# Softmax denominators handled four units at a time, with DMA gathering and spreading them

## The chip, the cores and the metric

The kernel runs on one core of a Trainium2 chip. The metric is device time in microseconds (us). Three runs of the kernel before took 253.03, 253.61 and 254.1 us; the median is 253.61. Engines are named as the profile names them: PE (matrix), DVE (vector), ACT (scalar), POOL (GpSimd), SP (the engine that issues the DMAs). PSUM is the memory that PE writes, SBUF the working memory.

## What is computed

An adaLN block on 2048 tokens of width 512. A sliding-window attention with 32 heads of 16 dimensions comes first, then a token-mixing MLP of width 1792:

```python
mod = (silu(c) @ w_mod).reshape(1, 6, 1, 512)        # sa, ca, ga, sb, cb, gb
h = layernorm(x) * (1 + ca) + sa
q, k, v = split(h @ wqkv)                            # 32 heads of 16
p = softmax(mask(q @ k.T / 4))                       # a token sees itself and the 255 before it
x = x + ga * ((p @ v) @ wo)
h = layernorm(x) * (1 + cb) + sb
u = gelu(einsum('bsd,sf->bdf', layernorm(h), w1) + b1)
x = x + gb * (einsum('bdf,fs->bds', u, w2) + b2).T
```

## The kernel before, in words

**Tiling.** Tokens go in four groups G of 512, each of two halves H of 256 tokens (so H runs from 0 to 7). The 32 heads go in four sets g8 of eight. A *unit* is one half with one head set; there are 32 units. The scores of the units are cut into 75 *chunks*; units share chunks, five chunks for a pair of units (L438). The names below are the operation names in the code, and they are used in the prediction.

**One chunk** (L1161). `S`: PE writes scores for four heads into three PSUM banks (`pss`, one buffer) and a fourth (`psb`, two buffers). `EA`, `EB`: ACT takes the exponential of `pss` (1536 columns) and of `psb` (512) into the SBUF tile `et` (`E_BUFS` = 7 buffers). `M`: DVE multiplies parts of `et` by a mask.

**One unit** (L1229, L1265). When its last chunk is masked, `AV`: PE makes the weighted values and, with a block of constants (`ones_bd`, L303), the denominators. Both go into one PSUM bank `po`: columns 0 to 255 the values, columns 256 to 511 the denominators, each repeated over the 16 partitions of its head. Then `ln` and `rz` on ACT give 1/denominator as exp(-ln z) in the SBUF tile `lz` (128x256 each), and `OT` on DVE multiplies the values in PSUM by it. `OT` frees the bank. There are three such banks (`od`), shared with every projection and with the MLP.

**Around it.** `proj(G)` (L866): the layernorm of x (`l1st` statistics on DVE, `l1ag` eight small steps on POOL, `xn` the normalization), a transposing DMA `xt`, scale and shift `h1T`, then matmuls k, q, v. Each result is copied out of PSUM (`ke`, `qe`, `ve`) and laid out by `kk` (K), `vo` and `vp` (V; `vp` after a DMA `vx`). `post(G)` (L1023): the output projection `wo` on PE, `x2` adds x, `l2st`, `l2ag`, `n2` (normalize), `m2` (two tensor operations: times cb, plus sb), `l3st`, `l3ag`, `hb` (normalize again, into the tiles `hb` that the MLP reads). `partials()` (L1090): the pieces `p` of the first MLP matmul that need only the tokens of groups 0 and 1: `p0` to `p19` need the `hb` tiles of group 0, `p20` to `p55` also those of group 1. `pe` and `pd` take them out of PSUM. `tail()` (L1328): the rest of the first matmul (`u`), the activation, and the second matmul (`py`), whose weights are loaded behind everything else.

**What sets the order.** All operations are created first and numbered in the order of creation. The list `ORDER` (L62) is a permutation of these numbers, and every engine executes its own operations in that order, SP's DMA issues too. Operations that may go on more than one engine take the engine under which `CHOSEN` (L118) lists their number. Both lists are constants. The costs in the code (the numbers in `op(...)`) choose PSUM banks and cost nothing at run time.

**Broadcast vectors** (L541). `bc`: for each of four vectors, four matmuls with a stationary tile in which silu(c) is repeated over 128 columns, into a bank of its own. `bce`: one DVE instruction each into `bc_ga`, `bc_cb1`, `bc_sb`, `bc_gb`.

Of the kernel before, what the change touches and what calls it, by code (L numbers as in the profile page):

```python
# [22 lines left out]
NG = 4  # L23
# [36 lines left out]
E_BUFS = 7  # L60
LOG = None
ORDER = [  # L62
# [54 lines left out]
]  # L117
CHOSEN = {  # L118
    "ACT": [
        47, 48, 50, 51, 74, 82, 1062,  # L120
    ],
    "DVE": [
# [5 lines left out]
    ],  # L128
    "POOL": [
# [86 lines left out]
def kernel(  # L216
# [324 lines left out]
    for n, (v, dst) in enumerate(((2, bc_ga), (4, bc_cb1), (3, bc_sb), (5, bc_gb))):  # L541
        def e_bc(n, v=v):
            if n == 0:
                box["bc", v] = bank([P, D], F32, "ps_b")
# [890 lines left out]
```

## Time and profile before

| | us |
|---|---|
| median of three runs | 253.61 |
| span of the profiled execution, first to last instruction | 252.3 |
| PE busy | 235.3 |
| DVE busy | 205.4 |
| ACT busy | 179.5 |
| POOL busy | 126.3 |

The run list gives no time of its own for the profiled execution. Its span lies 1.3 us under the median of the runs, and a run's time also holds what lies around the span. Nearly all instructions go through one helper line (L256), so groups in the profile are told apart by their tiles: `et<-pss` is `EA`, `et<-psb` is `EB`, `et<-et,maskt` is `M`, `lz<-po` is `ln`, `lz<-lz` is `rz`, `OT<-po,lz` is `OT`, `KT<-kb,mask_par` is `kk`, `VT<-vb` and `VT<-vs` are `vo` and `vp`. A view of windows gives the busy time of each engine in stretches of the span. The granted PE clock is 1.00 in all of them.

### The profile page before, as it was taken

To read this page: it belongs to the slowest core of one execution; us is meant where nothing else is said; L and a number is where in the kernel's file an instruction comes from. 1 tells how busy PE (TensorE), PEld (TensorE's weight loads), DVE (VectorE), ACT (ScalarE), POOL (GpSimd) and SP (SyncE) were. 2 spreads that over 40 slices of the span, in tenths; PEclk is the share of its full clock that TensorE was granted. 3 is DMA by queue.
4 is the path that set the end of the run, shared out by engine and by line. 5 is a ranking of instruction groups with operands and counts; after the bars stand their busy time and mean duration, and the time that the engine had idled before them with its cause. 6 is when DMAs were issued, how large, how long until landed. Compare 5 with 4: busy or idle time off the path is not lost.

```text
span 252.3 us, 9189 instructions
## 1 busy us (share of the span) xinstructions
PE 235.3 (93%) x3949; PEld 126.0 (50%) x3949; DVE 205.4 (81%) x408; ACT 179.5 (71%) x254; POOL 126.3 (50%) x228
## 2 busy tenths in 40 slices
PE   7988888899987889999999999999999999999995
PEld 2656644445554544555546454556444444444443
DVE  5499998989989998999897999999978764444443
ACT  4699998999999999999999999997147510000000
POOL 8268968795899989845886348173000000000000
PEclk9999999999999999999999999999999999999999
DMA  6999364356055200003401536314999201111111
GB/s 200 323 351 294 48 47 86 44 70 187 3 74 112 53 23 3 4 3 104 131 3 45 155 82 189 105 44 113 343 388 386 108 22 43 44 52 52 42 44 42
DMA packets 42625, 28.13 MB, mean 111 GB/s; under 512 B 12376, under 2 KB 38488, under 8 KB 42584
## 3 DMA queue, kind: packets, MB, share of 16 engines
q1 hardware_dynamic: 42576, 27.54, 39.4%
q8 instruction: 31, 0.51, 0.9%
q14 instruction: 10, 0.08, 0.1%
q10 hardware_dynamic: 8, 0.00, 0.0%
HBM read 22.03 MB, written 2.10 MB: 96 GB/s over the span
## 4 chain that ended last, share of the span: by engine, by line
PE 52%; ACT 24%; DVE 7%; DMA 5%; issue 5%; POOL 4%; SPq 1%; POOLq 0%; DVEq 0%
ACT et L256 20%; PE py L256 19%; PE pu L256 16%; PE po L256 5%; PE pss L256 5%; ACT lz L256 3%; PE pa L256 3%; DMA x<-in_A_x_dram 2%; DVE et L256 2%; DMA h1T<-xn 2%; DMA wmod<-in_w_mod_dram 1%; POOL h1T L256 1%; PE pq L256 1%; DVE st L256 1%; PE pk L256 1%
## 5 line engine op out<-in xcount | busy, mean ns | idle before, releaser
L256 ACT ACTIVATE et<-pss 128x1536 bf16<-128x1536 f32 x75 | 110.7, 1476 | 2.8 <-PE psb L256 2.3
L256 PE MATMUL py<-guT,w2r 128*128 128x512 bf16 (+2 forms) x238 | 48.7, 366 | 0.0
L256 ACT ACTIVATE et<-psb 128x512 bf16<-128x512 f32 x75 | 46.9, 626 | 0.0
L256 DVE TENSOR_TENSOR et<-et,maskt 128x1024 bf16<-128x1024 bf16 (+2 forms) x79 | 46.4, 603 | 0.1
L256 PE MATMUL pu<-hb,w1s 128*32 128x512 bf16 (+1 forms) x302 | 39.0, 380 | 0.2 <-DVE QT L256 0.2
L256 PEld LDWEIGHTS <-w2r 128*128 128x128 bf16 x238 | 22.8, 98 | 26.1 <-issue 0.3
L256 PE MATMUL pss<-QT,KT 32*128 32x64 bf16 (+3 forms) x720 | 29.9, 230 | 6.2 <-ACT et L256 3.5
L256 PE MATMUL po<-et,VT 128*32 128x64 bf16 (+3 forms) x960 | 32.2, 234 | 1.3 <-DVE kb L256 0.6
L256 PE MATMUL po<-et,ones_bd 128*32 128x256 bf16 (+3 forms) x624 | 31.7, 268 | 0.0
L256 PEld LDWEIGHTS <-KT 32*128 32x128 bf16 x960 | 17.1, 92 | 28.5 <-issue 24.6
L256 DVE TENSOR_TENSOR otile<-py,xr 128x512 bf16<-128x512 f32 (+2 forms) x17 | 11.2, 660 | 24.4 <-PE py L256 24.2
L256 POOL TENSOR_SCALAR KT<-kb,mask_par 128x512 bf16<-128x512 bf16 (+1 forms) x36 | 25.0, 707 | 11.4 <-DVE kb L256 11.1
L256 PE MATMUL psb<-QT,KT 32*128 32x64 bf16 (+3 forms) x240 | 29.3, 231 | 0.0
L256 PEld LDWEIGHTS <-VT 128*32 128x32 bf16 x960 | 20.8, 96 | 13.2 <-issue 4.7
L256 PE MATMUL pk<-h1T,wqkv 128*32 128x512 bf16 (+4 forms) x228 | 21.1, 340 | 2.4 <-DVE OT L256 1.0
L256 DVE BATCH_NORM_STATS2 st<-x 128x6 f32<-128x512 bf16 x32 | 21.5, 680 | 2.1 <-DMA x<-in_A_x_dram 2.1
L256 PEld LDWEIGHTS <-wqkv 128*32 128x32 bf16 (+1 forms) x350 | 15.3, 96 | 12.7 <-issue 4.7
L256 PEld LDWEIGHTS <-w1s 128*32 128x32 bf16 (+1 forms) x302 | 14.1, 97 | 15.0 <-issue 1.5
L256 PE MATMUL pv<-wqkv,h1T 128*32 128x512 bf16 (+2 forms) x202 | 17.1, 348 | 1.3 <-DVE OT L256 0.7
L256 PE MATMUL pu<-hb,w1r 128*128 128x512 bf16 (+1 forms) x96 | 17.9, 380 | 0.0
L256 PE MATMUL pa<-wod,OT 128*32 128x512 bf16 (+1 forms) x136 | 17.2, 381 | 0.0
L256 PEld LDWEIGHTS <-ones_bd 128*32 128x32 bf16 x624 | 15.8, 97 | 0.1
(109 smaller groups left out, 350.1 us busy)
## 6 DMA issues: line engine op xcount, KB each, us to landing
w2r<-in_B_w_dram SPq DMA_DIRECT2D x14, 512.0 KB, 10.2
w1s<-in_B_w_dram SPq DMA_DIRECT2D x19, 256.0 KB, 4.0
w1r<-in_B_w_dram SPq DMA_DIRECT2D x9, 256.0 KB, 4.3
x<-in_A_x_dram SPq DMA_DIRECT2D x16, 128.0 KB, 5.2
wmod<-in_w_mod_dram SPq DMA_DIRECT2D x4, 512.0 KB, 7.8
out_dram<-otile SPq DMA_DIRECT2D x15, 128.0 KB, 1.7
wmod<-in_w_mod_dram SPq DMA_DIRECT2D x4, 256.0 KB, 3.9
wqkv<-in_A_wqkv_dram SPq DMA_DIRECT2D x4, 256.0 KB, 5.7
```

Of the source, the lines that this page charges most:

```text
L256: ins = call(*args, **kwargs)
```

## The change

Units are finished in batches. All but the last two units go through it: seven batches of four units and one of two.

- `ev` (DVE or ACT) copies the whole bank, values and denominators, to the SBUF tile `ev` (128x512 float32, six buffers) and frees the bank.
- `zg` (a DMA) gathers the eight distinct rows of denominators of the unit into eight rows of the tile `zc`.
- After the fourth `zg` of a batch, one `ln` and one `rz` on ACT work on the 32 rows of `zc`.
- `zb` (a DMA for each unit) spreads each of the eight rows over 16 partitions, back into `ev`.
- `OT` (DVE or POOL) multiplies the two halves of `ev`, both in SBUF.

The last two units keep `ln`, `rz` and the multiply from PSUM. The four broadcast vectors are made by sixteen matmuls of 32 columns, four side by side, into one bank; one `bce` scales them, and four DMAs `bb` spread them over the partitions. To make room in SBUF, `et` has six buffers in place of seven, some tiles move to pools that are released earlier, and the last four `hb` tiles are made only when the weights of the projections are released.

`ORDER` and `CHOSEN` are new throughout. Counted by name, these operations change their number or their engine:

| operation | before | after |
|---|---|---|
| `OT` | DVE 32 | DVE 10, POOL 22 |
| `ev` | none | DVE 28, ACT 2 |
| `ln` and `rz` | ACT 64 | ACT 20 |
| `zg`, `zb`, `bb` | none | SP 64 |
| `bce` | DVE 4 | DVE 1 |
| `xn` | DVE 7, POOL 9 | DVE 4, POOL 12 |
| `n2` | DVE 8, POOL 8 | DVE 6, POOL 10 |
| `m2` | DVE 12, POOL 4 | DVE 11, POOL 5 |
| `vo` | DVE 2, POOL 10 | POOL 12 |
| `vp` | POOL 16 | DVE 1, POOL 15 |
| `kk` | DVE 1, POOL 18 | DVE 2, POOL 17 |
| `pe` | DVE 13, ACT 1 | DVE 11, ACT 3 |
| `ve` | DVE 16 | DVE 15, ACT 1 |

```diff
-E_BUFS = 7
+E_BUFS = 6
+EV_BUFS = 6
...
+    zc = const.tile([P, HQ], F32, name="zc")
...
+    def e_bc(n):
+        if n == 0:
+            box["bc"] = bank([P, D], F32, "ps_b")
+        for k in (2 * n, 2 * n + 1):
+            for i, (v, _) in enumerate(vectors):
                 te.matmul(
-                    box["bc", v][:], lhsT=sT_rep[:, k, :], rhs=wmod[:, k, v * D : (v + 1) * D],
-                    start=(k == 0), stop=(k == ND - 1),
+                    box["bc"][32 * i : 32 * i + 32, :], lhsT=sT_rep[:, k, :], rhs=wmod[:, k, v * D : (v + 1) * D],
+                    start=(k == 0), stop=(k == ND - 1), tile_position=(0, 32 * i), skip_group_check=True,
                 )
...
+        def e_bb(e, n=n, dst=dst):
+            dma.dma_start(out=dst[:], in_=bcs[32 * n : 32 * n + 32, :].unsqueeze(1).to_broadcast([32, ND, D]))
...
     def finish(unit, i):
...
+        def e_o(e):
+            ENGINE[e].tensor_tensor(
+                out=OT[G % 2][g8][:, (Hh % 2) * HQ : (Hh % 2 + 1) * HQ],
+                in0=(unit["ps"] if direct else unit["ev"])[:, 0, :], in1=unit["ev"][:, 1, :], op=ALU.mult,
+            )
...
+        def e_ev(e):
+            e_new()
+            copy(e, unit["ev"][:], unit["ps"][:])
+
+        def e_zg(e):
+            dma.dma_start(out=zc[rows, :], in_=unit["ev"][0 : P : DH, 1, :])
+
+        def e_zb(e):
+            dma.dma_start(out=unit["ev"][:, 1, :], in_=zc[rows, :].unsqueeze(1).to_broadcast([8, DH, HQ]))
+
+        a = op("ev", {"DVE": 0.6, "ACT": 0.5}, 0.6, e_ev, deps=[av], pos=i + LZ_POS)
+        unit["avs"][0].frees = [a]
+        g = op("zg", "SP", 0.5, e_zg, deps=[a], pos=i + LZ_POS, extra=0.2)
...
+        def e_bln(e):
+            ac.activation(out=zc[own, :], in_=zc[own, :], func=ACT.Ln)
+
+        def e_brz(e):
+            ac.activation(out=zc[own, :], in_=zc[own, :], func=ACT.Exp, scale=-1.0)
...
+            z = op("zb", "SP", 0.5, e_spread, deps=[b], pos=at + LZ_POS, extra=1.2)
+            spread.append(z)
+            d = mult_ops[u["H"], u["g8"]] = op("OT", {"DVE": 0.34, "POOL": 0.8}, 0.34, e_mult, deps=[z], pos=at + OT_POS)
```

From the new `ORDER`, the parts that the prediction uses. POOL, from the `l3ag` of group 0 to that of group 1: `l3ag0 hb1 hb2 OT10 kk15 OT15 vp12 vp13 OT12 vo8 kk14 vo9 l2ag1 n26 n24 n25 m26 kk16 m24 vo11 OT16 vp15 kk18 vo10 kk17 vp14 l3ag1 hb5 hb4`. The same stretch before: `l3ag0 kk13 kk12 hb3 vp10 hb0 kk14 vo6 hb2 vp11 l2ag1 n24 n27 m26 m27 l3ag1 vo8 kk15 hb5 vp13 hb7`. PE after: `... S41 AV48 AV49 p6 S42 p7 p0 p1 S43 ...` and `... S60 p20 AV70 p21 p44 S61 ...`; before: `... S42 AV45 AV46 p0 p1 S43 ...` and `... S55 ... S56 p20 p21 ...`. Numbers behind a name count its operations from 0 in the order of creation (so `S42` is the 43rd chunk).

More of the change, by code (lines that the diff above doesn't have):

```diff
@@ L274 @@
     xres = [xpool.tile([P, D], BF, name=f"x{t}") for t in range(NT)]
-    hb = [xpool.tile([P, D], BF, name=f"hb{t}") for t in range(NT)]
+    hb = [xpool.tile([P, D], BF, name=f"hb{t}") for t in range(NT - ND)]
     identity = const.tile([P, P], BF, name="identity")
@@ L306 @@
     nc.gpsimd.memset(ones_bd[KB:P, DH : 2 * DH], ZSCALE)
-    nothing = const.tile([P, D], BF, name="nothing")
-    nc.vector.memset(nothing[:], 0.0)
     late = ctx.enter_context(tc.tile_pool(name="late", bufs=2))
@@ L318 @@
     VT = [kvpool.tile([P, 8, DH, 2 * DH], BF, name=f"VT{r}") for r in range(3)]
-    work = att.enter_context(tc.tile_pool(name="work", bufs=2))
     epool = att.enter_context(tc.tile_pool(name="epool", bufs=E_BUFS))
@@ L335 @@
     modw = tc.alloc_tile_pool(name="modw", bufs=1, side="right")
-    warm = nothing
+    warm = nothing = modw.tile([P, D], BF, name="nothing")
+    nc.vector.memset(nothing[:], 0.0)
     wmod = modw.tile([P, ND, 6 * D], BF, name="wmod")
@@ L473 @@
     sT = modw.tile([P, ND], BF, name="sT")
-    sT_rep = modw.tile([P, ND, P], BF, name="sT_rep")
+    sT_rep = modw.tile([P, ND, 32], BF, name="sT_rep")
+    bcs = modw.tile([P, D], BF, name="bcs")
+    bc_fix = modw.tile([P, 2], F32, name="bc_fix")
+    nc.gpsimd.memset(bc_fix[:, 0:1], 1.0)
+    nc.gpsimd.memset(bc_fix[0:32, 0:1], ZSCALE)
+    nc.gpsimd.memset(bc_fix[:, 1:2], 0.0)
+    nc.gpsimd.memset(bc_fix[32:64, 1:2], 1.0)
     box = {}
@@ L504 @@
     o5.frees = [o6]
-    o_rep = op("sTrep", "DVE", 0.35, lambda e: ve.tensor_copy(
-        out=sT_rep[:], in_=sT[:].unsqueeze(2).to_broadcast([P, ND, P])), deps=[o6], pos=-6, ready=15.0)
+    o_rep = op("sTrep", "DVE", 0.15, lambda e: ve.tensor_copy(
+        out=sT_rep[:], in_=sT[:].unsqueeze(2).to_broadcast([P, ND, 32])), deps=[o6], pos=-6, ready=15.0)
     def e_fm(k):
@@ L652 @@
     transposed = {}
+    placed = []
     def proj0():
@@ L781, in e_kb @@
             def e_kb(e):
-                box["kb", g8] = work.tile([P, D], BF, name="kb", tag=kb_tag, bufs=1)
+                box["kb", g8] = wpool.tile([P, D], BF, name="kb", tag=kb_tag, bufs=1)
                 copy(e, box["kb", g8][:, 0 : 2 * P], box["kq", g8][:, 0, :])
@@ L823, in e_ve @@
             def e_ve(e):
-                box["vb", tb] = work.tile([P, 2, 256], BF, name="vb", tag=vb_tag, bufs=1)
+                box["vb", tb] = wpool.tile([P, 2, 256], BF, name="vb", tag=vb_tag, bufs=1)
                 copy(e, box["vb", tb][:], box["v", tb][:])
@@ L953, in e_ke @@
                 else:
-                    box["kb", g8] = work.tile([P, D], BF, name="kb", tag=kb_tag, bufs=1)
+                    box["kb", g8] = wpool.tile([P, D], BF, name="kb", tag=kb_tag, bufs=1)
                     copy(e, box["kb", g8][:], box["k", g8][:])
@@ L982, in e_ve @@
             def e_ve(e):
-                vb = box["vb", tb] = work.tile([P, 2, 256], BF, name="vb", tag=vb_tag, bufs=1)
+                vb = box["vb", tb] = wpool.tile([P, 2, 256], BF, name="vb", tag=vb_tag, bufs=1)
                 copy(
@@ L989, in e_vx @@
             def e_vx(e):
-                vs = box["vs", tb] = work.tile([P, 256], BF, name="vs", tag=vs_tag, bufs=1)
+                vs = box["vs", tb] = wpool.tile([P, 256], BF, name="vs", tag=vs_tag, bufs=1)
                 dma.dma_start(out=vs[0:KB, :], in_=box["vb", tb][KB:P, 0, :])
@@ L1011, in v @@
             b = op("vp", {"POOL": 0.78, "DVE": 0.45}, 0.78, lambda e: e_vp(e, False), deps=[vx] + war + zeros[r3], pos=pos)
+            placed.extend([own, b])
             slot(vb_tag, ve_op, own, vx)
@@ L1102, in e_rel @@
             box["B"] = ctx.enter_context(tc.tile_pool(name="partB", bufs=1, side="right"))
+            hb.extend(box["B"].tile([P, D], BF, name=f"hb{t}") for t in range(NT - ND, NT))
         for n in range(NF // 2):
@@ L1267, in finish @@
         av = av_ops[G, g8] = unit["avs"][-1]
-        lz_tag = turn("lz")
-        def e_ln(e):
-            unit["lz"] = late.tile([P, HQ], F32, name="lz", tag=lz_tag, bufs=1)
-            ac.activation(out=unit["lz"][:], in_=unit["ps"][:, 1, :], func=ACT.Ln)
-        def e_rz(e):
-            ac.activation(out=unit["lz"][:], in_=unit["lz"][:], func=ACT.Exp, scale=-1.0)
+        tag = turn("ev", EV_BUFS)
+        direct = Hh == 2 * NG - 1 and g8 >= 2
+        members = box.setdefault("batch", [])
@@ L1277, in e_o, with e_new @@
+        def e_new():
+            unit["ev"] = kvpool.tile([P, 2, HQ], F32, name="ev", tag=tag, bufs=1)
         def e_o(e):
-            ve.tensor_tensor(
+            ENGINE[e].tensor_tensor(
                 out=OT[G % 2][g8][:, (Hh % 2) * HQ : (Hh % 2 + 1) * HQ],
-                in0=unit["ps"][:, 0, :], in1=unit["lz"][:], op=ALU.mult,
+                in0=(unit["ps"] if direct else unit["ev"])[:, 0, :], in1=unit["ev"][:, 1, :], op=ALU.mult,
             )
-        a = op("ln", "ACT", 0.26, e_ln, deps=[av], pos=i + LZ_POS)
@@ L1284, in finish, with e_ln, e_rz @@
-        b = op("rz", "ACT", 0.31, e_rz, deps=[a], pos=i + LZ_POS)
-        d = mult_ops[Hh, g8] = op("OT", "DVE", 0.34, e_o, deps=[b], pos=i + OT_POS)
-        unit["avs"][0].frees = [d]
-        slot(lz_tag, a, d)
+        if direct:
+            def e_ln(e):
+                e_new()
+                ac.activation(out=unit["ev"][:, 1, :], in_=unit["ps"][:, 1, :], func=ACT.Ln)
+            def e_rz(e):
+                ac.activation(out=unit["ev"][:, 1, :], in_=unit["ev"][:, 1, :], func=ACT.Exp, scale=-1.0)
+            a = op("ln", "ACT", 0.26, e_ln, deps=[av], pos=i + LZ_POS)
+            b = op("rz", "ACT", 0.31, e_rz, deps=[a], pos=i + LZ_POS)
+            d = mult_ops[Hh, g8] = op("OT", "DVE", 0.34, e_o, deps=[b], pos=i + OT_POS)
+            unit["avs"][0].frees = [d]
+            slot(tag, a, d)
+            return
@@ new lines, in finish @@
+        unit["avs"][0].frees = [a]
+        g = op("zg", "SP", 0.5, e_zg, deps=[a], pos=i + LZ_POS, extra=0.2)
+        members.append((unit, i, tag, a, g, e_o, e_zb))
+        if len(members) < (2 if Hh == 2 * NG - 1 else 4):
+            return
+        own = slice(32 * (box["batches"] % 4), 32 * (box["batches"] % 4) + 8 * len(members))
+        def e_bln(e):
+            ac.activation(out=zc[own, :], in_=zc[own, :], func=ACT.Ln)
+        def e_brz(e):
+            ac.activation(out=zc[own, :], in_=zc[own, :], func=ACT.Exp, scale=-1.0)
@@ new lines, in finish @@
+        n = box["batches"]
+        a = op("ln", "ACT", 0.26, e_bln, deps=[m[4] for m in members], pos=i + LZ_POS)
+        slot(f"zc{n % 4}", members[0][4])
+        b = op("rz", "ACT", 0.31, e_brz, deps=[a], pos=i + LZ_POS)
+        spread = []
+        for u, at, tag, first, g, e_mult, e_spread in members:
+            z = op("zb", "SP", 0.5, e_spread, deps=[b], pos=at + LZ_POS, extra=1.2)
+            spread.append(z)
+            d = mult_ops[u["H"], u["g8"]] = op("OT", {"DVE": 0.34, "POOL": 0.8}, 0.34, e_mult, deps=[z], pos=at + OT_POS)
+            slot(tag, first, d)
@@ L1289 @@
+        tenants[f"zc{n % 4}"] = spread
+        box["batches"] += 1
+        box["batch"] = []
     for G in range(NG):
```

38 lines of the change are left out of this document (17 added, 21 removed), and 128 rows, old and new, of tables (CHOSEN, ORDER).

## The prediction

> **What bounds the kernel now.** I read the share of busy time first, then three stretches, then the chain that ended last to see which engine carries each.
>
> ```profile
> span 252.3 us, 9189 instructions
> PE 235.3 (93%) x3949; PEld 126.0 (50%) x3949; DVE 205.4 (81%) x408; ACT 179.5 (71%) x254; POOL 126.3 (50%) x228
> ```
>
> ```profile
> core 0: us, PE busy (x) PEld busy (x) DVE busy (x) ACT busy (x) POOL busy (x), PEclk, DMA share, GB/s
> 24.30:118.50 94.20, 84.54 (x2078) 47.66 (x2078) 89.18 (x175) 92.72 (x126) 76.89 (x125) 1.00 0.31 56
> 118.50:172.50 54.00, 53.53 (x1152) 28.68 (x1152) 49.97 (x93) 53.37 (x73) 33.04 (x58) 1.00 0.34 94
> ```
>
> ```profile
> 116.98 1.46 ACT et L256
> ...
> 118.88 1.83 PE pu L256 x8
> ...
> 178.50 22.45 PE pu L256 x104
> ```
>
> Until 118.5 us the chain runs through ACT's exponentials and ACT is idle for 1.5 us of 94.2. Behind 118.5 it runs through PE, which is idle for 0.5 us of 54, and from 178.5 PE alone carries it. So the end moves with PE: it is later by what PE waits more, earlier by what it waits less or has less to do. PE is idle for 94.2 - 84.5 = 9.7 us in the first stretch, and little is to be had elsewhere. But DVE is idle there for only 5.0 us, and POOL for 17.3.
>
> **ACT: relief, 44 instructions fewer.** Rows of ACT in time show what one costs.
>
> ```profile
> 59.22 1.45 ACT L256 ACTIVATE et<-pss 128x1536 bf16<-128x1536 f32 x1
> 60.57 0.59 ACT L256 ACTIVATE et<-psb 128x512 bf16<-128x512 f32 x1
> 61.16 1.45 ACT L256 ACTIVATE et<-pss 128x1536 bf16<-128x1536 f32 x1
> 62.51 0.38 ACT L256 ACTIVATE lz<-po 128x256 f32<-128x256 f32 x1
> 62.77 0.60 ACT L256 ACTIVATE et<-psb 128x512 bf16<-128x512 f32 x1
> 63.25 0.43 ACT L256 ACTIVATE lz<-lz 128x256 f32<-128x256 f32 x1
> 63.56 1.46 ACT L256 ACTIVATE et<-pss 128x1536 bf16<-128x1536 f32 x1
> ```
>
> A chunk without `ln` or `rz` takes 61.16 - 59.22 = 1.94 us, one with both 63.56 - 61.16 = 2.40. A pair costs 0.46 us of the chunk loop. Of the 20 pairs that start in the first stretch four remain as batches: ACT could run 16 x 0.46 = 7.4 us ahead there. That is the most that this part can give, since the second stretch is PE's.
>
> **PE: 3 us less.**
>
> ```profile
> L256 PE MATMUL ps_b<-wmod,sT_rep 128*128 128x512 bf16 x16 | 4.1, 380 | 0.0
> L256 PE MATMUL pu<-hb,w1s 128*32 128x512 bf16 x200 | 13.5, 380 | 0.0
> ```
>
> The sixteen broadcast matmuls take 4.1 us. In the form with 32 columns, four side by side, 200 took 13.5 us, so sixteen take 1.1. They lie in the first stretch, where PE has idle time: between 0 and -3 us on the path. I take 0, because by what follows PE waits for POOL behind them.
>
> **DVE: 3.5 us more, late.**
>
> ```profile
> L256 DVE TENSOR_TENSOR OT<-po,lz 128x256 bf16<-128x256 f32 x32 | 13.2, 415 | 2.4 <-ACT lz L256 1.9
> L256 DVE COPY part<-pu 128x512 f32<-128x512 f32 x13 | 8.8, 678 | 0.3 <-PE pu L256 0.2
> ```
>
> `part<-pu` is the same copy as `ev`. Instructions overlap by some 0.07 us, so one takes 0.61 of the engine, and an `OT` 0.35. 28 copies add 17.1, 22 multiplies that leave take 7.7 away, and the rest (three `bce`, three `xn`, two `pe`, two `n2`, a `ve`, a `m2`, two `vo` gone; a `kk`, a `vp`, a `cp`, a `qe` added, at similar sizes) takes 5.9 away. Net +3.5. By the new queue the work ahead of the mask of chunk 50 is the same within 0.5 us, and the surplus falls behind it, on DVE's 4.0 us of idle time in the second stretch, where DVE would be as full as PE. On the path between 0 and 3.5. I take 0, because PE's own surplus behind chunk 60 (below) leaves DVE time; the upper end stays for the range.
>
> **POOL: the part that I think decides.** The rows are for 24.8 to 123.0 us, from the end of the first statistics on POOL to the end of `l3ag1`.
>
> ```profile
> 24.80:92.50 67.70, 59.57 (x1501) 33.63 (x1496) 64.10 (x129) 66.23 (x93) 56.60 (x95) 1.00 0.41 70
> 92.50:123.00 30.50, 28.97 (x652) 15.71 (x654) 28.94 (x54) 30.48 (x40) 22.67 (x39) 1.00 0.18 50
> ```
>
> ```profile
> L256 POOL TENSOR_SCALAR KT<-kb,mask_par 128x512 bf16<-128x512 bf16 x14 | 11.6, 841 | 0.1
> L256 POOL TENSOR_SCALAR xn<-x,rs,nm 128x512 bf16<-128x512 bf16 x9 | 8.4, 931 | 0.2
> L256 POOL COPY VT<-vs 64x256 bf16<-64x256 bf16 x16 | 7.1, 441 | 3.6 <-DMA vs<-vb 3.0
> L256 POOL COPY VT<-vb 64x256 bf16<-64x256 bf16 x13 | 6.2, 477 | 1.8 <-DVE vb L256 1.5
> L256 POOL TENSOR_SCALAR h<-x,rs,nm 128x512 bf16<-128x512 bf16 x5 | 4.7, 940 | 0.1
> L256 POOL TENSOR_TENSOR h<-h,bc_cb 128x512 bf16<-128x512 bf16 x3 | 4.2, 1385 | 3.4 <-DVE h L256 3.3
> L256 POOL TENSOR_TENSOR h<-h,bc_sb 128x512 bf16<-128x512 bf16 x3 | 3.6, 1184 | 0.2
> L256 POOL TENSOR_SCALAR hb<-h,rs,nm 128x512 bf16<-128x512 bf16 x3 | 2.3, 765 | 0.2
> L256 POOL TENSOR_TENSOR mv<-st 128x8 f32<-128x8 f32 x6 | 1.8, 299 | 3.8 <-DVE st L256 3.6
> ```
>
> Busy in the two stretches: 56.6 + 22.7 = 79.3 us of 98.2. The trace has no multiply of 128x256 float32 on POOL. A two-input operation takes 0.30 us at 8 columns and 1.18 at 512, so about 0.74 at 256: I take 0.75, with bounds 0.6 and 1.18 (as if float32 cost by bytes). Ahead of the end of `l3ag1` the new POOL queue has, more than the old: 11 `OT` (8.3), 3 `kk` of two instructions (5.0), 6 `vo` (5.7), 3 `vp` (2.6), 3 `xn` (2.8), a `m2` (2.6), a `n2` (0.9), one `hb` fewer (-0.8). Together 27.1, so 106.4 us of work: `l3ag1` cannot end before 24.8 + 106.4 = 131.2, against 123.0 now. Then come `hb5` and `hb4` (1.5): 132.7 with POOL never idle. In the same stretch POOL is now idle for 18.9 us. The rows name 3.3 + 3.6 for DVE's `h` and statistics and 3.0 + 1.5 for pieces of V; 7.5 are other DMAs and gaps between small steps. A POOL that is later than now finds DVE's work ready, but the gaps stay, and it waits for `zb` too: I take 8 us of idle time (bounds 0 and 18.9), so `hb4` at 140.7.
>
> Who waits: `p20`, which needs `hb4` to `hb7`, stands on PE right behind `S60`, and all further scores stand behind `p20`; on DVE `hb6` and `hb7` stand ahead of the mask of chunk 58.
>
> ```profile
> 102.32 1.45 ACT L256 ACTIVATE et<-pss 128x1536 bf16<-128x1536 f32 x1
> ```
>
> ```profile
> 140.84 1.45 ACT L256 ACTIVATE et<-pss 128x1536 bf16<-128x1536 f32 x1
> ```
>
> These are the exponentials of chunks 42 and 60, counted from 0 in the trace. `S60` is done when the second starts, so at today's pace PE stands at `p20` at 141, and `hb4` at 140.7 allows no gain there. The same holds earlier: through `l3ag0` the new queue has 7 `OT`, a `kk`, a `m2`, 3 `vo`, a `vp` and 3 `xn` more, 16.0 us; 24.8 + 56.6 + 16.0 + 1.5 for `hb1`, `hb2` = 98.9 without idle time, and with 5 of the 11.1 us that are idle now 103.9. `p6`, which needs them, stands ahead of `S42`, whose exponential starts at 102.3 now: a stall of 2 us, more if PE arrives early. So POOL takes back what ACT gives. And behind `S60` the new order leaves PE more to do. Ahead of it stand four pieces each of `p` and `wo` fewer, and two pieces of k and two `AV` more. A piece is two full matmuls; the 104 from 178.5 took 22.45 us, 0.22 each, so a piece is 0.43, and an `AV` is about the same: 8 x 0.43 - 4 x 0.43 = 1.7 us more left at that point than now.
>
> [...]
>
> ```profile
> L256 DVE TENSOR_TENSOR et<-et,maskt 128x1024 bf16<-128x1024 bf16 x43 | 31.8, 742 | 0.1
> 123.88 1.36 POOL L256 TENSOR_SCALAR KT<-kb,mask_par 128x512 bf16<-128x512 bf16 x2
> ```
>
> [...]
>
> **DMAs.**
>
> ```profile
> VT<-nothing SPq DMA_DIRECT2D x2, 512.0 KB, 4.7
> vs<-vb SPq DMA_DIRECT2D x24, 32.0 KB, 1.9
> ```
>
> `zg` is like `vs<-vb`, 1.9 us; `zb` moves 128 KB, between 1.9 and 4.7, and I take 2.5, near the smaller. From the last copy of a batch to its first product: 1.9 + 0.4 + 0.4 + 2.5 + 0.75 = 6 us (8.2 by the upper end). The first `wo` that needs the product stands between five and ten chunks of 1.94 us behind, which covers it. In the last full batch it is barely covered: 0 to 2 us, I take 0. SP issues 64 DMAs more, some 0.5 us each, in a queue that mostly waits. Six `et` buffers cost nothing: PE makes a unit's `AV` right behind its last chunk, ahead of the chunk that reuses the tile.
>
> **Sum.** At `p20` +0.9: `hb4` at 140.7 and then DVE's `hb6` and `hb7` (0.6 each on DVE, as an `ev`, at most) make 141.9 against 141; the wait at `p6` and ACT's and PE's relief lie ahead of this point and are swallowed by it. Then +1.7 of PE work. 252.3 + 2.6 = 254.9 of span, and with the 1.3 us by which the median stands above the span 256.2 us.
>
> **The rivals.**
> 1. *POOL keeps up, ACT's relief counts.* If two-input float32 on POOL costs 0.6 and POOL's waits vanish, `hb4` comes at 131 and gates nothing (106.4 less 11 x 0.15, from 24.8: 131). Then DVE is the next limit in the first stretch: 89.2 us of work; at ACT's present 98.5% that is 90.6 of 94.2, a gain of 3.6, less 1 in the second stretch: 253.6 - 2.6 = 251.0. For it: each engine that bounds now is 98 to 99% busy. It decides if `hb4` lands before 137.
> 2. *POOL is worse.* At 1.18 per product, 11 x 0.43 = 4.7 us more ahead of `l3ag1`, and all of it passes to PE: 256.2 + 4.7 = 260.9. It decides from `hb4` at 143 on.
> 3. *It changes nothing.* The second stretch is PE's with the same work; POOL's lateness and ACT's gain cancel: 253.6, within 1.2.
>
> **How the numbers follow.** My forecast of 256.2, own range 254.9 to 259: 0.47. Rival 1: 0.25. Rival 2: 0.13. Rival 3: 0.15. About 0.5% (1.3 us) is what a measurement of this kernel can tell from no change. Faster 0.25, same 0.15, slower 0.6. The range runs from 250.5 to 261, which leaves out the far ends of rivals 1 and 2.
>
> **What would show it.** Right: POOL busy above 90% from 25 to 135 us, `l3ag1` ending near 138, PE idle before `pu<-hb` near chunks 42 and 60 with POOL or DVE's `hb` as releaser, ACT idle in the first stretch, chunk 60 not earlier than now. `ev` copies of 0.68 us, products on POOL of 0.75. Wrong: POOL with long idle stretches, chunk 60 starting before 138, or PE waiting for DMA `ev<-zc`.

## The result and the profile after

Four runs of the changed kernel took 281.46 to 289.03 us, with a median of 285.64. Two of the four, the profiled one of 289.03 us among them, were disturbed, so from here on a time is the median of a kernel's undisturbed runs, 282.76 us for this one, and the rows below show somewhat more loss than that. The kernel before took 253.86 us in the same session. The change makes the kernel 1.115 times as long, 95% interval 1.109 to 1.121. The forecast was 256.2, in a range of 250.5 to 261.0: the sign was right, the size far off.

The page of the changed kernel, share of busy time:

```profile
span 287.1 us, 9114 instructions
PE 244.4 (85%) x3830; PEld 127.0 (44%) x3853; DVE 220.7 (77%) x403; ACT 174.2 (61%) x213; POOL 149.3 (52%) x261
```

The busiest engine, PE, is at 85%, from 93%. POOL was to be busy above 90% of the time from 25 to 135 us; it is busy for 85.1 of these 110 us, 77%. The two windows that the prediction showed of the kernel before (the first number after the stretch is its length, then busy time by engine):

```profile
24.30:118.50 94.20, 75.04 (x1715) 41.39 (x1713) 80.34 (x141) 76.22 (x85) 77.61 (x123) 0.95 0.39 72
118.50:172.50 54.00, 43.04 (x907) 22.14 (x909) 46.33 (x73) 39.67 (x44) 34.10 (x55) 0.91 0.30 61
```

ACT, 92.7 of 94.2 us busy before, is now idle for 18 us of the first stretch, and PE, 53.5 of 54 before, for 11 of the second. The granted clock, 1.00 before, is 0.95 and 0.91. What they wait for, from the view of waits (us in total, times, longest us), and from the chain that ended last (start us, us, what):

```profile
ACT et L259 <- PE psb L259: 30.8, 26, 4.3
POOL OT L259 <- DMA ev<-zc: 24.1, 11, 7.2
...
ACT zc L259 <- DMA zc<-ev: 6.4, 3, 3.2
...
DVE OT L259 <- DMA ev<-zc: 4.2, 3, 2.5
```

```profile
111.85 7.11 DMA ev<-zc
...
149.62 4.48 DMA ev<-zc
...
158.01 3.97 DMA zc<-ev
...
191.56 6.23 DMA ev<-zc
...
204.91 5.97 DMA ev<-zc
```

POOL waits 24.1 us for the spread, in its own queue, and what it has to do behind a product (values laid out for the next group, normalizations) is held back with it. ACT waits 6.4 us for the gathering DMA. The spread stands on the chain in pieces of 4.5 to 7.1 us, a gathering with 4.0; none was forecast there. The prediction had named this as a sign of being wrong: POOL with long idle stretches. The exponentials show most of the loss. In the kernel before ACT waited this long for scores:

```profile
ACT et L256 <- PE psb L256: 2.3, 5, 0.7
```

28.5 us more, of the 34.8 by which the span of this execution is longer (287.1 against 252.3).

### The profile page after: what moved, and what is told of

The parts are those of the page before. It is cut to its first block, busy times and chain, and to the rows that moved or that the text cites. A ratio compares the mean times of both kernels' runs of the same rounds, so it can differ in the third digit from the quotient of the medians.

```text
span 287.1 us, 9114 instructions
## 1 busy us (share of the span) xinstructions
PE 244.4 (85%) x3830; PEld 127.0 (44%) x3853; DVE 220.7 (77%) x403; ACT 174.2 (61%) x213; POOL 149.3 (52%) x261
## 4 chain that ended last, share of the span: by engine, by line
PE 35%; DMA 10%; DVE 7%; ACT 5%; issue 3%; POOL 3%; SPq 1%; POOLq 0%; ACTq 0%; DVEq 0%
PE py L259 17%; PE pu L259 10%; DMA ev<-zc 8%; ACT et L259 4%; PE pa L259 4%; PE pss L259 2%; DVE et L259 2%; PE po L259 2%; POOL h L259 1%; DMA zc<-ev 1%; DVE h L259 1%; SPq L259 1%; DVE ev L259 1%; DVE st L259 1%; DVE part L259 1%
## 5 line engine op out<-in xcount | busy, mean ns | idle before, releaser
L259 ACT ACTIVATE et<-pss 128x1536 bf16<-128x1536 f32 x75 | 108.7, 1449 | 32.9 <-PE psb L259 30.8
L259 DVE TENSOR_TENSOR et<-et,maskt 128x1024 bf16<-128x1024 bf16 (+2 forms) x79 | 51.0, 662 | 4.7 <-ACT et L259 4.6
L259 ACT ACTIVATE et<-psb 128x512 bf16<-128x512 f32 x75 | 44.5, 593 | 0.1
L259 PE MATMUL pu<-hb,w1s 128*32 128x512 bf16 (+1 forms) x266 | 40.9, 403 | 2.6 <-DVE ev L259 1.0
L259 PE MATMUL po<-et,VT 128*32 128x64 bf16 (+3 forms) x960 | 33.9, 238 | 8.0 <-POOL VT L259 3.2
L259 PE MATMUL pss<-QT,KT 32*128 32x64 bf16 (+3 forms) x720 | 31.5, 238 | 9.8 <-ACT et L259 6.9
L259 POOL TENSOR_TENSOR OT<-ev 128x256 bf16<-128x256 f32 x22 | 18.4, 847 | 24.3 <-DMA ev<-zc 24.1
L259 DVE TENSOR_TENSOR otile<-py,xr 128x512 bf16<-128x512 f32 (+2 forms) x17 | 11.2, 660 | 24.8 <-PE py L259 23.1
L259 PEld LDWEIGHTS <-wqkv 128*32 128x32 bf16 (+1 forms) x290 | 15.8, 100 | 20.3 <-issue 11.7
L259 PE MATMUL pa<-wod,OT 128*32 128x512 bf16 (+1 forms) x147 | 19.4, 400 | 6.2 <-POOL OT L259 3.3
L259 DVE COPY ev<-po 128x512 f32<-128x512 f32 x28 | 18.9, 678 | 1.7 <-PE po L259 1.6
L259 PE MATMUL pq<-h1T,wqkv 128*32 128x512 bf16 (+2 forms) x104 | 14.5, 401 | 6.0 <-DVE kb L259 4.0
```

The costliest lines, as they stand in the source:

```text
L259: ins = call(*args, **kwargs)
```

## The experiments

Theory A: the spread DMA is slow in itself. Theory B: SP's queue is held by it. Theory C: the prediction's, POOL's added work. Theory D: the broadcast vectors come late. Later came P (products on POOL), Q (the batching's work on DVE), R (the places in the new order) and B6 (the sixth `et` buffer). Medians are in us, with the ratio to the kernel before, run beside it (253.3 to 254.0 in all sessions), and its 95% interval. The runs without DMAs leave out the division, other than e2_act_units and e9_old_finish, and those with 16 columns leave out most of the values too.

| run | median | ratio |
|---|---|---|
| changed kernel | 282.76 | 1.115 (1.109 to 1.121) |
| e1_no_dma | 265.32 | 1.046 (1.039 to 1.052) |
| e2_act_units | 269.51 | 1.062 (1.056 to 1.068) |
| e3_rows_apart | 267.94 | 1.055 (1.051 to 1.060) |
| e14_rows_two_apart | 268.77 | 1.060 (1.057 to 1.062) |
| e4_zb_from_act | 287.61 | 1.128 (1.121 to 1.136) |
| e6_before_bc | 255.23 | 1.005 (1.002 to 1.008) |
| e5_no_dma_small_pool | 263.22 | 1.037 (1.032 to 1.041) |
| e8_ev_act | 267.60 | 1.053 (1.048 to 1.057) |
| e7_ev_act_ot_dve | 268.83 | 1.058 (1.050 to 1.066) |
| e10_short_copies | 262.74 | 1.035 (1.033 to 1.038) |
| e16_short_copies_seven | 263.10 | 1.037 (1.033 to 1.041) |
| e9_old_finish | 288.54 | 1.139 (1.133 to 1.144) |
| e11_old_order | 327.49 | 1.290 (1.284 to 1.295) |
| e12_old_order_no_dma | 291.43 | 1.149 (1.145 to 1.152) |
| e13_old_order_dve_pool | 290.49 | 1.144 (1.141 to 1.147) |
| e15_before_six_et | 289.50 | 1.142 (1.135 to 1.149) |
| e17_old_order_seven | 260.26 | 1.029 (1.024 to 1.033) |
| e18_old_order_seven_short | 255.28 | 1.006 (1.003 to 1.009) |

### The DMAs taken away, and their rows moved apart

```diff
-            dma.dma_start(out=zc[rows, :], in_=unit["ev"][0 : P : DH, 1, :])
+            pass
-            dma.dma_start(out=unit["ev"][:, 1, :], in_=zc[rows, :]...to_broadcast([8, DH, HQ]))
+            pass
```

> The changed kernel without the gathering and the spreading DMAs: zc is set to 1 once, ln and rz of a batch work on it, and the product multiplies the unit's values by the sums that ev holds already. So the division is left out; the order, the copies and all products on POOL stay. Theory A (the spread DMA: it reads eight neighbouring partitions, a batch takes 5 to 11 us, and POOL, DVE and ACT stand behind it in their queues): 250 to 258 us, POOL idle before OT under 3 us in place of 24. Theory B (SP's queue: four spreads hold SP for 5.5 us and the loads behind them come late): 250 to 258 us too. Theory C (the prediction's: POOL has 27 us more to do ahead of l3ag1, the DMAs only shift it): 275 us or more, POOL busy above 90% from 25 to 135 us.

265.32: the DMAs, both together, cost 17.4 us of the 29. Not all of it, as A and B had it, and not little, as C had it.

The next one keeps both DMAs and changes only in which rows of `zc` a unit's denominators lie:

```diff
-        rows = slice(32 * (batches % 4) + 8 * len(members), ... + 8)      # 8 neighbours
+        rows = slice(32 * (batches % 4) + len(members), ... + 32, 4)      # every fourth
```

> The changed kernel with the eight rows of a unit four partitions apart in zc (its batch's 32 rows are interleaved) in place of eight neighbours; zc starts as 1. Same bytes, same number of DMAs, same order. Theory A: a spread reads from 29 partitions' width in place of 8, its packets get shorter than 100 ns (150 before), and the time falls to 262 to 275 us. Theory B with a fixed issue cost: 283 to 289 us, SP still held 5.5 us by a batch. Theory C: 283 to 289 us.

267.94: of the 17.4 us, 14.8 go when the eight rows are not neighbours, with the same bytes and the same number of DMAs. The third version takes every second row (two units share sixteen):

```diff
+        at2 = 32 * (batches % 4) + 16 * (len(members) // 2) + len(members) % 2
+        rows = slice(at2, at2 + 15, 2)
```

> The changed kernel with the eight rows of a unit two partitions apart in zc: a spread reads from a width of 15 partitions, between 8 (285.6 us, 150 ns a packet) and 29 (267.9 us, 46 ns a packet). Theory A (many reads out of few neighbouring partitions hold each other up): between the two, 70 to 110 ns a packet, 270 to 281 us. If only the direct neighbour matters: as e3_rows_apart, 266 to 270 us. If the width doesn't matter and e3_rows_apart was faster for another reason: 283 to 288 us.

268.77, nearly all of the gain of e3_rows_apart. The time lies where the rival put it that only the direct neighbour matters (266 to 270 us); the packets below lie where theory A put them (84 ns, between 70 and 110), and they decide against that rival, since the rows four apart are faster again. How long POOL's products waited for the spread (the view of the tile `zc`: who waited, us, times), in the changed kernel, with rows two apart and with rows four apart:

```profile
  POOL OT L259: 24.1, 11
```

```profile
  POOL OT L259: 8.6, 5
```

```profile
  POOL OT L259: 3.0, 1
```

The trace also has each packet. Where one spread ran alone, the median of its 128 packets of 1 KB and its time from issue to last packet were, with rows 1, 2 and 4 apart, and beside them a batch of four spreads:

```
rows apart   ns a packet   one spread alone   third batch: from first issue to last packet
1            150           4.1 us             9.0 us
2            84            2.7 us             6.5 us
4            46            2.0 us             4.2 us
```

So in these three kernels a packet took longer the closer together the partitions lie that are read: 46, 84 and 150 ns, 1.8 times as long for each halving of the distance. From first to last packet the lone spreads took 0.75, 1.4 and 2.8 us, about twice as long each time. What in the chip makes the difference, no run here shows.

The time hardly falls from two apart to four apart (268.77 to 267.94); POOL's wait for the spread had by then fallen from 24.1 to 8.6 us, and falls to 3.0.

### SP's queue

How long one batch of four spreads holds SP, rows of SP in the changed kernel and with rows four apart:

```profile
66.56 5.44 SPq L259 DMA_DIRECT2D ev<-zc  x4
```

```profile
64.01 2.71 SPq L259 DMA_DIRECT2D ev<-zc  x4
```

A slow spread also holds its issuer (SP, for 5.44 us a batch in place of 2.71), so e3_rows_apart alone does not tell theory B from theory A. In the next run the spreads are issued by ACT:

```diff
-            dma.dma_start(out=unit["ev"][:, 1, :], in_=zc[rows, :]...)
+            ac.dma_start(out=unit["ev"][:, 1, :], in_=zc[rows, :]...)
```

> The changed kernel with the spreading DMAs issued on ACT's queue in place of SP's; everything else as it is. Theory B (four spreads hold SP for 5.5 us, and the loads and gatherings behind them come late): SP's queue is free, the loads come in time, and the time falls by over half of the 20 us that the DMAs cost, to 268 to 276 us, ACT's queue paying some 0.6 us for each of 30. Theory A (the data itself is late, since each packet out of eight neighbouring partitions takes 150 ns): 280 us or more, POOL still waiting for the spread some 20 us, and ACT blocked in SP's place.

287.61, no better. The waits in that kernel:

```profile
POOL OT L259 <- DMA ev<-zc: 32.3, 11, 8.1
```

SP no longer issued the spreads, and POOL waited 32.3 us for them instead of 24.1. So B falls as far as SP's queue goes: the data is late with SP relieved, and A stands. ACT was held in SP's place (up to 2.77 us for one issue), and what that costs by itself was not separated.

### ACT's relief and the broadcast vectors

```diff
-            ac.activation(out=zc[own, :], in_=zc[own, :], func=ACT.Ln)
+            for u, *_ in batch:
+                ac.activation(out=u["ev"][:, 1, :], in_=u["ev"][:, 1, :], func=ACT.Ln)
```

> The changed kernel without both DMAs; at the place of a batch's ln and rz ACT makes ln and rz for each of its units on that unit's own ev (128 x 256 each), so the division is made and the batching on ACT alone is undone. ACT has about 22 pairs more at 0.46 us each, some 10 us, and the first stretch is ACT's. Theories A and B: 255 to 265 us, no engine waiting for a DMA of ev. Theory C: 275 us or more.

Against e1_no_dma it only adds 44 instructions on ACT (ln and rz of each unit on its own `ev`). ACT's busy time rose from 174.1 to 184.7 us, 0.48 a pair (forecast 0.46), the time by 4.2, to 269.51, which lies between the ranges of the theories. So ACT's relief is worth 4.2 us within the new order without DMAs, of the 7.4 that were its most.

The other part that can stand alone is the broadcast vectors, put into the kernel before:

```diff
+                for i, w in enumerate((2, 4, 3, 5)):
+                    te.matmul(box["bc", v][32 * i : 32 * i + 32, :], ..., tile_position=(0, 32 * i))
...
+            for i, d in enumerate((bc_ga, bc_cb1, bc_sb, bc_gb)):
+                dma.dma_start(out=d[:], in_=bcs[32 * i : 32 * i + 32, :]...to_broadcast([32, ND, D]))
```

> The kernel before with one part of the change alone: the sixteen 32-column broadcast matmuls into one bank, one scaling on DVE and four spreading DMAs to the broadcast vectors, at the places of the fourth vector's matmuls and copy. Theories A, B and C: 250 to 255 us, this part is worth at most its 3 us of PE. Theory D (the broadcast vectors come late by DMA and hold the normalizations): 258 us or more, with PE or DVE waiting for bc tiles.

255.23, slower by 0.2 to 0.8%. In the changed kernel the sixteen column tiles take 1.0 us of PE as forecast (1.1), here 1.5, and none of the saving reaches the end; the part costs about 1.3 us. The granted clock goes with that. In the profiled run it is 0.51 from 35.5 to 39.0 us, the only such stretch, and PE had been busy for 1.48 of the 3.5 us ahead of it, against 3.03 in the kernel before, which makes part of its broadcast matmuls there. The two of the ten runs with a granted clock of 1.000 took 253.43 and 253.67, no more than the kernel before; the eight at 0.987 to 0.993 took 254.76 to 256.19. No instruction waits for the tile `bc_sb`, whose DMA took 3.9 us to land.

### What is left without DMAs: 11.7 us

In e1_no_dma POOL is nearly as full as forecast. The window from 24.8 us to where POOL starts its two `hb` of group 1:

```profile
24.80:144.80 120.00, 104.97 (x2399) 57.62 (x2395) 113.78 (x199) 107.42 (x120) 109.51 (x173) 0.99 0.26 54
```

POOL works 109.5 us and idles 10.5. With the two `hb` (1.7) that makes 111.2 of work and an end at 146.5; the forecast had 107.9, 8 idle and 140.7. The numbers look like a confirmation. The next run makes POOL's products 16 columns long:

```diff
+            cols = 16 if e == "POOL" else HQ
-                in0=unit["ev"][:, 0, :], in1=unit["ev"][:, 1, :], op=ALU.mult,
+                in0=unit["ev"][:, 0, 0:cols], in1=unit["ev"][:, 1, 0:cols], op=ALU.mult,
```

> As e1_no_dma (no gathering, no spreading, no division), and in addition POOL's 22 products multiply 16 of the 256 columns; the rest of OT is 0, so most of their values are left out. e1_no_dma left 11.7 us of loss. In it POOL's product took 0.88 us, and DVE's operations on SBUF were longer than before: the mask 0.647 us against 0.603, the product 0.635 against 0.415 from PSUM. Theory P (POOL's products are the rest, by their own 0.5 us each that goes here and by what they cost DVE): 253 to 258 us, the mask back at 0.61. Theory Q (DVE's 28 copies of 0.68 us are the rest): 262 us or more.

```profile
24.80:144.80 120.00, 103.72 (x2407) 58.11 (x2411) 115.17 (x200) 107.99 (x121) 104.10 (x173) 0.99 0.27 53
```

263.22. POOL has 5.4 us less to do here, and the `hb` start at 144.9 all the same: POOL only waits longer for DVE's statistics (23.5 us in all, in place of 15.8). POOL's load did not set `hb4`. Theory P gets 2.1 us of the 11.7.

Theory Q gets as little. Half of DVE's copies moved to ACT, and then half of POOL's products moved to DVE, both with rows four apart:

```diff
+for n in (145, 153, 193, 223, 366, 396, 436, 466, 608, 638, 678, 708, 850, 880):
+    CHOSEN["DVE"].remove(n)
+    CHOSEN["ACT"].append(n)
+for n in (160, 164, 230, 403, 471, 643, 713, 717, 885, 889, 925):      # e7_ev_act_ot_dve only
+    CHOSEN["POOL"].remove(n)
+    CHOSEN["DVE"].append(n)
```

> e3_rows_apart with every second copy ev that DVE makes moved to ACT (14 of 28). DVE has 14 x 0.61 = 8.5 us less, ACT 14 x 0.6 = 8.4 more, which is about what the batching had taken from it. Theory Q (DVE's copies are the rest of the loss): 259 to 263 us, from 267.9. Theory P (POOL's products are): 265 to 269 us.

> e8_ev_act with every second product that POOL makes moved to DVE as well (11 of 22): POOL has 11 x 0.88 = 9.7 us less, DVE 11 x 0.42 = 4.6 more. Theory P: 257 to 262 us, the mask on DVE near 0.62 us. Theory Q: 262 to 266 us, above e8_ev_act, since DVE has more to do again.

267.60 and 268.83 against 267.94: no change in the first, and none clear of the noise in the second (the interval of its ratio, 1.050 to 1.066, covers that of e3_rows_apart, 1.051 to 1.060). So both predicted gains stay out. Then the copies and all batched products were cut to 16 columns:

```diff
-            copy(e, unit["ev"][:], unit["ps"][:])
+            copy(e, unit["ev"][:, :, 0:16], unit["ps"][:, :, 0:16])
```

> As e5_no_dma_small_pool, and the 30 copies ev and all batched products are 16 columns long, on DVE too: the division and most of the values are left out, and DVE has some 28 x 0.45 = 13 us less. What the batching costs DVE and POOL is nearly gone, the places stay. Theory Q: 250 to 256 us. Theory R: 260 to 263 us, next to e5_no_dma_small_pool's 263.2.

262.74. With neither the DMAs nor most of the batching's work, 9 us are still lost. ACT's waits in that kernel:

```profile
ACT et L259 <- PE psb L259: 12.0, 17, 2.1
```

12.0 us against 2.3 before, and 12.3 in e1_no_dma with all that work: the scores come late with that work and without it. That points to theory R, the places.

### The order, and the buffer that it was made for

Four runs tried the places directly. In the first, ln, rz and product of each unit stand at the place of its copy in the new order; in the second, the batching stands in the old order; the third and fourth are the second without DMAs. The edit of the first, and for the others new lists `ORDER` and `CHOSEN` made from the old ones (too long to show). In the first the DMAs and the later products of the batched units are left out too:

```diff
-            copy(e, unit["ev"][:], unit["ps"][:])
+            ac.activation(out=unit["ev"][:, 1, :], in_=unit["ps"][:, 1, :], func=ACT.Ln)
+            ac.activation(out=unit["ev"][:, 1, :], in_=unit["ev"][:, 1, :], func=ACT.Exp, scale=-1.0)
+            ve.tensor_tensor(out=OT[G % 2][g8][...], in0=unit["ps"][:, 0, :], in1=unit["ev"][:, 1, :], op=ALU.mult)
```

> The new order with the old finish: at the place of a unit's copy ACT makes ln and rz from PSUM for that unit and DVE multiplies from PSUM; no copies, no gathering, no spreading, no products on POOL. All other operations stay at the places and on the engines of the changed kernel. Division made. Theory Q (the work that the batching puts on DVE and POOL is what is left of the loss without DMAs, 11.7 us): 251 to 257 us. Theory R (the places are: the output projection of group 1 stands behind score chunks 43 to 46 in place of 36 to 41, since it allows for the spread, and hb4 to hb7 and p20 follow from it; work moved to POOL for it too): 260 us or more.

> The batching with rows four apart in the order of the kernel before: every operation that both have stands at its old place and on its old engine (ORDER and CHOSEN are made from the old lists); copies stand at the place of the old ln, half on DVE and half on ACT, ln and rz of a batch one chunk behind its last copy, products on DVE three chunks behind, and only what must wait for them (the output projections and what follows) moves back, by some six chunks. Six et buffers. Division made. Theory R (other places and engines cost, the batching's work does not): 253 to 259 us. Theory Q: 260 to 268 us, DVE above 97% busy from 25 to 140 us.

> As e1_no_dma (no gathering, no spreading, no division), but in the order of the kernel before: every operation that both have stands at its old place and on its old engine; the copy stands at the place of the old ln, half of the copies on DVE and half on ACT, the product on DVE at the place of the old product (nothing has to be waited for), ln and rz of a batch one chunk behind its last copy. Only the release of the projections' weights comes later, since it has more to wait for. Theory R (the places cost what is left without DMAs): 250 to 257 us, ACT idle between its first and last exponential under 6 us in place of 15.2. Theory Q (the work): 260 us or more.

> As e12_old_order_no_dma, with all 30 copies on DVE and every second product on POOL, which is how the changed kernel shares the batching's work. DVE has 15 x 0.61 = 9 us more than in e12_old_order_no_dma, less some 6 for products, ACT 8 less. Theory R: within 3 us of e12_old_order_no_dma. Theory Q: 262 us or more.

288.54, 327.49, 291.43 and 290.49. By the letter the first speaks for R, the second fits neither, the third speaks for Q and the fourth fits both, but all four are far beyond what either can explain. Waits of the first and of the fourth:

```profile
DVE OT L259 <- ACT ev L259: 39.0, 26, 3.1
```

```profile
ACT et L254 <- PE po L254: 28.1, 28, 2.2
```

The first says nothing on Q or R: DVE's products wait for ACT, whose ln stands in places made for a copy on DVE. The fourth tells what had been overlooked.

An exponential waits for PE's `po`: it may write its `et` tile only when the weighted values (`AV`) that read it are done, and with six tiles in place of seven the old order has `AV` too late for that. The forecast had put the sixth buffer at nothing. The buffer was taken from the kernel before alone; in `ORDER` 25 wide exponentials, a narrow one and a score that stood ahead of the `AV` that frees their tile are placed behind it:

```diff
-E_BUFS = 7
+E_BUFS = 6
```

> The kernel before with six et buffers in place of seven, nothing else: 25 of the 75 wide exponentials, a narrow one and a score move back by 2 to 9 places in the order, to stand behind the AV that frees their buffer. Theory B6 (the seventh et buffer is worth much, and the new order pays for its loss with AV and projections in worse places): 265 to 290 us, ACT waiting for po. My prediction's step that six buffers cost nothing: 253 to 256 us.

```profile
PE pss L254 <- ACT et L254: 41.1, 49, 1.6
ACT et L254 <- PE po L254: 31.7, 34, 1.9
```

289.50: one buffer is worth 36 us in the old order, more than the whole change cost (29). The tiles `ev` took its room (six of 2 KB per partition; an `et` tile is 4 KB). So the order had to be made anew, with `AV` earlier. Whether seven buffers help in the new order (the shortened copies leave room), and what the old order costs with seven (`E_BUFS = 7`, `EV_BUFS = 4`), with the work and with it cut to 16 columns:

> e10_short_copies with seven et buffers (room from copies' tiles of 16 columns): the new order is laid out for six, so only slack can come back. Division and most values left out, as there. Theory B6: 255 to 262 us, at least 1 under e10_short_copies. If the buffers don't bind in the new order: 262 to 264 us.

> e12_old_order_no_dma with seven et buffers and four ev: the old order and the batching's work (copies half on DVE and half on ACT, products on DVE from SBUF), no DMAs, no division. Theory B6 with theory R: 250 to 258 us, from 291.4 with six. Theory Q (the work costs): 260 us or more, ACT not waiting for po but PE and ACT for DVE.

> e17_old_order_seven with copies and batched products of 16 columns, as in e10_short_copies: the old order with seven et buffers and the batching's work nearly gone (division and most values left out). If the 7 us that e17_old_order_seven lost are the batching's work on DVE and ACT: 249 to 255 us, and the new order laid out for six buffers costs the difference to e10_short_copies' 262.7. If something else in the old order as rebuilt costs them (the later release of the projections' weights): 258 to 261 us.

263.10: a buffer given back to an order laid out for six helps nothing, and theory B6 misses here. 260.26 in the old order with the batching's work, just inside theory Q's range; 255.28 with that work cut short, just above the range for a loss by that work. DVE in the stretch of 94.2 us (24.3 to 118.5), with the work and without it:

```profile
24.30:118.50 94.20, 79.94 (x1994) 44.96 (x1990) 91.05 (x177) 89.49 (x103) 78.74 (x126) 0.98 0.29 58
```

```profile
24.30:118.50 94.20, 81.75 (x2090) 47.30 (x2097) 86.53 (x185) 89.96 (x108) 77.43 (x125) 0.98 0.31 62
```

With it DVE is busy 91.1 of 94.2 us, 97%, and without it 86.5, while ACT's busy time hardly differs (89.5 and 90.0); that agrees with theory Q for this order. The runs then stack up, each step one difference of medians:

```
old order, seven et, work cut short (e18)    255.3    +1.7 to before
new order, six et, work cut short (e10)      262.7    +7.5
with the work (e1)                           265.3    +2.6
with DMAs, rows apart (e3)                   267.9    +2.6
with DMAs, rows neighbours (changed kernel)  282.8   +14.8
```

The step of 7.5 changes the lists `ORDER` and `CHOSEN` together, so other engines make the shortened copies and products and some other operations too (POOL is busy 144.4 us in place of 130.2). That the new lists cost it is shown; that they cost it because the order was laid out for six buffers is argued from e15_before_six_et and e16_short_copies_seven, not shown, and which of its places cost it stays open. One such place can be seen in e10_short_copies, where PE has pieces of q and k of the last group and an `AV` between score chunks 51 and 53, each waiting for DVE, 3.1 us in a stretch of 6 (rows of PE; in brackets idle time and what ended it):

```profile
127.33 0.29 PE L259 MATMUL po<-et,VT 128*32 128x128 bf16 x8 [0.72 <-DVE ev L259]
...
128.66 1.05 PE L259 MATMUL pk<-h1T,wqkv 128*32 128x512 bf16 x16 [0.93 <-DVE QT L259]
...
132.46 1.05 PE L259 MATMUL pq<-h1T,wqkv 128*32 128x512 bf16 x16 [1.43 <-DVE kb L259]
```

No version tried here beats the kernel before.

## Why the prediction was wrong, step by step

- **"`zb` ... I take 2.5, near the smaller", covered by five to ten chunks.** This is the step that failed: the sum put the DMAs at nothing on the path, and they cost 17.4 us, 14.8 of them by the place of the rows. A lone spread took 4.1 us from issue to last packet, inside the bounds, but the sum priced one spread, up to the first product, and a batch of four took 9.0. The prices came from other DMAs; here a packet out of eight neighbouring rows takes 150 ns, and 46 out of rows four apart. The cover failed too. I looked for who needs the product on PE, and the first to wait is the queue of the engine that makes it: POOL waits 24.1 us for the spread and DVE 4.2, and ACT waits 6.4 for the gathering. Which partitions a spread reads, I did not weigh.
- **The sign.** It came out as forecast, but not for the reason given: of the +2.6 us, 0.9 was PE's wait at `p20` for a late POOL, which the points below do not find, and 1.7 was PE's work behind it, which no run measured by itself. As far as the mechanism goes that is luck.
- **"SP issues 64 DMAs more, some 0.5 us each, in a queue that mostly waits."** The issue itself takes 0.61 to 0.67 us (median), and four slow spreads hold SP for 5.4. But with SP relieved of them in e4_zb_from_act the time does not fall.
- **"POOL: the part that I think decides."** The price was near (0.75 forecast; in the changed kernel a mean of 0.85 and a median of 0.73) and so was the work ahead of `hb4`, yet it decides nothing: with POOL lightened `hb4` stays at 144.9, and with DVE lightened too (e10_short_copies) it starts at 144.4. I had a lower bound for POOL and took it for the path. The output projections of group 1 stand behind score chunks 43 to 46 in the new order, 36 to 41 before, and POOL waits for statistics that come behind them; that `hb4` follows from their place is argued, since no run moved them alone.
- **The stall at `p20`.** It isn't there. In e10_short_copies the score chunk ahead of `p20` waits for ACT's exponential, and `p20` (`pu<-hb`) follows it without a wait, though the `hb` end only at 146.1, 0.5 us ahead of it. In the changed kernel the `hb` end at 162.9 and `p20` starts at 165.6; PE waits 3.2 us just ahead of that score chunk, for an exponential, and ACT had waited 2.7 for the gathering. Rows of e10_short_copies:

```profile
146.31 0.29 PE L259 MATMUL pss<-QT,KT 32*128 32x256 bf16 x3 [0.55 <-ACT et L259]
...
146.64 0.62 PE L259 MATMUL pu<-hb,w1s 128*32 128x512 bf16 x8
```

- **"Six `et` buffers cost nothing."** True in the trace of the changed kernel, where no exponential waits for `po`, and false as a step: the old order loses 36 us by it. A buffer's price is paid in the order that has to do without it.
- **"DVE ... Net +3.5."** Measured 12.4 (217.8 in e1_no_dma against 205.4). Durations changed. DVE's groups before, and then in e1_no_dma (busy us, mean ns):

```profile
L256 DVE TENSOR_TENSOR et<-et,maskt 128x512 bf16<-128x512 bf16 x32 | 14.3, 456 | 0.0
...
L256 DVE TENSOR_TENSOR h<-h,bc_sb 128x512 bf16<-128x512 bf16 x12 | 6.0, 500 | 0.4
```

```profile
L259 DVE TENSOR_TENSOR et<-et,maskt 128x1024 bf16<-128x1024 bf16 x43 | 33.8, 791 | 1.4 <-ACT et L259 1.4
L259 DVE COPY ev<-po 128x512 f32<-128x512 f32 x28 | 18.9, 679 | 1.0 <-PE po L259 0.6
L259 DVE TENSOR_TENSOR et<-et,maskt 128x512 bf16<-128x512 bf16 x32 | 15.6, 488 | 0.0
L259 DVE TENSOR_TENSOR h<-h,bc_sb 128x512 bf16<-128x512 bf16 x11 | 8.1, 740 | 0.4
L259 DVE TENSOR_TENSOR OT<-ev 128x256 bf16<-128x256 f32 x8 | 5.1, 635 | 0.0
```

  The wide mask went from 742 to 791 ns, `h` from 500 to 740, the product from 415 (PSUM) to 635 (SBUF). These have two inputs in SBUF. `ev`, out of PSUM, stayed at 679 as forecast. But some operations with one input in SBUF grew as well (`h1T` of 512 columns from 426 to 610). With POOL's products cut to 16 columns the wide mask stayed near 790 (792 in e10_short_copies), so, against theory P, it is not the length of those products that the mask pays for; why it grew stays open. The prediction's row of two `kk` in 1.36 us bears on none of this: it is shorter than two mean steps (2 x 0.84), and no mask runs on DVE meanwhile.
- **ACT and PE.** The prices of ln and rz (0.48 a pair against 0.46) and of the column tiles (1.0 us against 1.1) were right. ACT's relief was worth 4.2 us, and lay under everything else.
- **The rivals.** Rival 1 fails even where the DMAs and most of the work are gone: e18_old_order_seven_short, with ACT relieved, comes to 255.3, not 251. Rival 2 had the right sign and the wrong engine. No rival had a DMA on the path.

## What to carry to other kernels

Price a DMA by the partitions that it reads as well as by its bytes: here a packet of 1 KB took 150 ns out of neighbouring rows and 46 out of every fourth, and every fourth row took 15 us off the kernel with a change of one slice. And here the queue of the engine that waits for the data was the first thing it delayed. An in-order kernel's buffers and its order are one thing: before room is taken from a ring, find in the order how late each tile is freed. A lower bound on one engine's work that lands near the measured time proves nothing; lighten that engine and see whether the time moves.

## What was not expected of the hardware

The packets of a spread out of eight neighbouring partitions took 150 ns, out of rows two apart 84, four apart 46, for the same 1 KB. And the granted PE clock was lower behind a stall of PE: windows of the changed kernel around the second batch (the number behind POOL's is that clock):

```profile
60.00:65.00 5.00, 2.40 (x48) 1.02 (x44) 3.23 (x6) 1.79 (x4) 2.64 (x4) 1.00 0.12 31
65.00:70.00 5.00, 2.28 (x32) 0.77 (x36) 1.88 (x3) 2.69 (x4) 4.29 (x13) 0.58 0.50 126
70.00:75.00 5.00, 4.87 (x104) 2.44 (x100) 3.02 (x7) 2.90 (x5) 4.34 (x7) 0.74 0.44 88
```

PE is busy for less than half of ten microseconds, the clock falls to 0.58, and when work returns it is at 0.74 over the next five. From 65.8 to 72.6 us the trace has it at 0.50, though PE is busy for 4.9 of these 6.8 us. That the stall lowers the clock is my reading of these windows; no run shows it by itself. PE's busy time is 244.4 us, against 237.9 in e1_no_dma with the same matmuls: 6.5 us more. How much of that reaches the end of the kernel was not measured.
